# Order of three steps in a fused attention and SwiGLU kernel: Prelu and exp ahead of the copy of the sums over V, the bias ahead of a turn's last products

## Chip, cores and metric

The kernel runs on one core of one Trainium2 chip. The metric is device time in microseconds for one launch, the median of the runs; lower is better. TensorE is called PE in the profile, VectorE DVE, ScalarE ACT, GpSimd POOL and SyncE SP.

## The reference

```python
# q, k, v: (8, 8, 576, 64), batch x heads x sequence x head_dim, float32
scores = scale * np.matmul(q, k.transpose(0, 1, 3, 2))
kth = np.partition(scores, -top_k, axis=-1)[..., -top_k:-top_k + 1]   # top_k = 32
scores = np.where(scores >= kth, scores, -1000000000.0)
scores = scores - np.max(scores, axis=-1, keepdims=True)
attn = np.exp(scores)
attn = attn / (np.sum(attn, axis=-1, keepdims=True) + 1e-09)
attn_out = np.matmul(attn, v)
x = attn_out.transpose(0, 2, 1, 3).reshape(4608, 512)
g = x @ w_gate                                  # 512 x 1536
silu = g * (1.0 / (1.0 + np.exp(-g)))
out = (silu * (x @ w_val)) @ w_out              # 1536 x 512
```

## The kernel before

**Units.** Attention is cut into 160 units: for each of 8 batches five groups of query rows (four of 128, and a last one of 64), and for each group four pairs of heads. In the last group a unit has one search over both heads; in the others it has two, one for each head. The sequence of 576 is 4 x 128 + 64, so `J` is 4 and `qt == J` means the last group.

**The steps of unit n.** `scores` multiplies q by k on TensorE (tile `s`, L325, or L308 for the last group), and ScalarE copies the product out with the scale (`sc`, L330 or L315). `select` finds the 32 largest of a row on VectorE, with four rounds of MAX8 (L347) and three of MATCH_REPLACE8 (L351). `shift` makes the bias of the exponential on GpSimd, out of the largest and the 32nd maximum (L362); it waits for VectorE's last MAX8. `weigh` runs Prelu (L374, with the 32nd maximum) and exp (L379, with the bias and the row's sum into `tot`) on ScalarE. `normalize` takes the reciprocal of the sum on VectorE (L392, L393), and scales `e` by it on ScalarE (L397) for one head and on GpSimd (L399) for the other. `turn` transposes `e` on TensorE (`etps`, L412), and ScalarE copies the result out (`et`, L413). `values` multiplies two units' `et` by V on TensorE (`av`, L448), and ScalarE copies the sums into `xT` (L464), the input of the feed-forward part.

**Feeds.** The feed-forward part handles blocks of 256 tokens (`kb`), each once its `xT` is complete. `feed` multiplies `xT` by `w_gate` and `w_val` (`f`, L603; L516 for the first blocks, in halves), ScalarE and GpSimd make the gated product `h` (ScalarE L636 to L643, GpSimd L639 and L644), and seven groups of products with combinations of `w_out` and `h` follow (`y_ps`, `x_ps`, L669). GpSimd forms the combinations of `h` that these need (L676, L684, L689, L717); L676 and L689 write them over the block's `xT`. GpSimd also adds up the output (L656). Before that the weights are brought in and rounded by ScalarE, VectorE and GpSimd (L117 to L126), mixed in with the first 13 units or so.

**Turns.** The main loop runs over n, here called turn n. It writes the order of every engine by hand: a chain of dependencies at the end of the kernel keeps each engine's instructions as they are written, so an instruction that waits holds up all that is written behind it on its engine. Turn n searches unit n, weighs and normalizes unit n - 1, transposes unit n - 2, and in even turns takes the sums over V of units n - 4 and n - 3 and the scores of units n + 1 and n + 2. In between, `pieces(k)` puts in up to k pieces of a feed, as many as a budget (`credit`) allows. A feed's copies and products on ScalarE and GpSimd are kept in two lists (`on_act`, `on_pool`) and written out by `flush`, at fixed places of the turn and when a list has more than one entry.

**Around the change.** Turn n begins as follows: the budget is set, `flush(on_act)`, the bias of unit n - 1, `flush(on_pool)`, in even turns the scores of unit n + 1 (products and copies), the sums over V (products and the copy to `xT`), the products of the scores of unit n + 2, then Prelu and exp of unit n - 1, then the copies of the scores of unit n + 2. Two pieces follow, the transposes of unit n - 2, more pieces and the search, `normalize`, the rest of the search, and `pieces(6)` last. `finish_units` also starts the loads of V for the next batch, when the units are those of a last group.

**Buffers.** The score tiles, the transposes and the sums over V share five PSUM banks (pool `ps_t`), the feeds have three (`ps_f`). In an even turn the first four transposes of the turn write the bank of that turn's sums, so they wait for the copy to `xT`. `xT` has three buffers. A feed's first product of each group of four reads the first pair of heads, the third reads the third pair.

Of the kernel before, what the change touches and what calls it, by code (L numbers as in the profile page):

```python
# [25 lines left out]
def kernel(  # L26
# [214 lines left out]
    def load_v(i):  # L241
        b, hp = pairs[i]
        h = slice(2 * hp, 2 * hp + 2)
        vt = slabs.tile([P, 2, J, D], FP32, tag="v", name="v")
        v_last = vtail[i % NV]
        vl = vlast[i % NV]
        nc.sync.dma_start(
            vt[:].rearrange("p h j d -> p h (j d)"),
            v[b, h, 0:JP].rearrange("h (p j) d -> p h (j d)", j=J),
        )  # L250
        nc.sync.dma_start(v_last[P - R : P], v[b, h, JP:S].rearrange("h p d -> p h d"))
        for hh in range(2):
            o = hh * R
            nc.sync.dma_start(vl[o : o + R, o : o + R], v[b, 2 * hp + hh, JP:S])
        vs[i] = (vt, v_last, vl)
# [28 lines left out]
    def n_heads(qt):  # L284

        return 1 if qt == J else 2
# [70 lines left out]
    def shift(n):  # L357

        st = state[n]
        m, nh = st["m"], len(st["heads"])  # L360
        bias = small.tile([P, 2], FP32, tag="bias", name="bias")
        nc.gpsimd.tensor_tensor(  # L362
            bias[:, 0:nh], m[:, 0:nh, TOP_K - 1], m[:, 0:nh, 0], ALU.subtract
        )
        st["bias"] = bias

    def weigh(n):


        st = state[n]  # L370
        sc, m, e, heads, bias = st.pop("sc"), st.pop("m"), st["e"], st["heads"], st.pop("bias")
        tot = small.tile([P, 2], FP32, tag="tot", name="tot")
        for t, (hs, at) in enumerate(zip(heads, st.pop("source"))):
            nc.scalar.activation(  # L374
                e[:, hs], sc[:, at], AF.Prelu, bias=m[:, t, TOP_K - 1 : TOP_K], scale=-1.0,
                alpha=SMALL,
            )
        for t, hs in enumerate(heads):
            nc.scalar.activation(  # L379
                e[:, hs], e[:, hs], AF.Exp, bias=bias[:, t : t + 1], scale=-1.0 / SMALL,  # L380
                accum_out=tot[:, t : t + 1],
            )
        if n < AHEAD:
            nc.scalar.add(tot[:, 0 : len(heads)], tot[:, 0 : len(heads)], EPS)
        st["tot"] = tot
# [37 lines left out]
    def values(ns):  # L423

        b, qt, hp0 = units[ns[0]]
        last = qt == J
        ql = R if last else P
        assert hp0 % 2 == 0
        halves = [slice(0, R), slice(R, P)]
        av = ps_t.tile([P, 2, P], FP32, tag="t", name="av")  # L430
        for i, n in enumerate(ns):
            assert units[n] == (b, qt, hp0 + i)
            vt, v_last, vl = vs[b * NHP + hp0 + i]
            et = state.pop(n)["et"]
            for c in (*range(J), J) if last else (J, *range(J)):
                for hh in range(2):
                    d = slice(hh * R, (hh + 1) * R)
                    if c == J:
                        weights_ = v_last[:, hh, :] if last else vl[:, d]
                    else:  # L440
                        weights_ = vt[:, hh, c, :]
                    at = halves[hh ^ i] if last else None
                    moving = (
                        et[:, c, at]
                        if last
                        else et[:, c + (0 if c == J else hh * (J + 1)), :]
                    )
                    nc.tensor.matmul(  # L448
                        av[d, i, 0:ql],
                        weights_,  # L450
                        moving,
                        start=c == (0 if last else J),
                        stop=c == (J if last else J - 1),
                    )
        c0 = b * S + qt * P
        at = c0
        hps = slice(hp0, hp0 + len(ns))
        while at < c0 + ql:
            kb = at // BLK
            n_c = min((kb + 1) * BLK, c0 + ql) - at  # L460
            if kb not in xT:
                xT[kb] = ffn.tile([P, NHP, BLK], FP32, tag="xT", name="xT", bufs=3)
                done[kb] = 0
            nc.scalar.copy(  # L464
                xT[kb][:, hps, at - kb * BLK : at - kb * BLK + n_c],
                av[:, 0 : len(ns), at - c0 : at - c0 + n_c],
            )
            done[kb] += n_c * len(ns)
            at += n_c
# [299 lines left out]
    NU = len(units)  # L769
# [6 lines left out]
    def piece():  # L776

        if len(on_act) > 1:
            flush(on_act)
        if len(on_pool) > 1:  # L780
            flush(on_pool)
        for job in early_jobs[:]:
            cost = next(job, 0)
            if cost == 0:
                early_jobs.remove(job)
            elif cost is not None:
                return cost
        if early_jobs:
            return 0
        while True:  # L790
            if not current:
                if not todo or done.get(todo[0], 0) < tokens(todo[0], int(todo[0] >= HALVED)):
                    return 0
                flush(on_act)
                flush(on_pool)
                current.append(feed(todo.pop(0)))
            cost = next(current[0], 0)
            if cost == 0:
                current.pop()
                continue  # L800
            return cost or 0

    def fetch(n):

        b, qt, hp = units[n]
        i = b * NHP + hp
        if qt == 0:
            yield from prep(i)
        if qt == J and i + NHP < len(pairs):
            load(i + NHP)  # L810
# [16 lines left out]
    def scored(n):  # L827

        ahead = [n + 1] if n < 2 else [] if n % 2 else [n + 1, n + 2]
        return [m for m in ahead if m < NU and (units[m][1] < J or m % 2 == 0)]  # L830

    def valued(n):

        behind = [] if n % 2 else [n - 4, n - 3]
        return [m for m in behind if 0 <= m < NU]

    def pieces(n):
        for _ in range(n):
            if credit[0] >= 1:
                credit[0] -= piece()  # L840

    def run(steps):
        for _ in steps:
            pass

    def finish_units(ns):
        values(ns)
        for n in ns:
            b, qt, hp = units[n]
            if qt == J and b + 1 < B:  # L850
                load_v((b + 1) * NHP + hp)
# [14 lines left out]
    no = iter(())  # L866
    TURN = 2
    due, steps = [2.0], []
    for n in range(NU + 3):
        nh = n_heads(units[n][1]) if n < NU else 1  # L870
        topk = select(n) if n < NU else no
        norm = normalize(n - 1) if 0 <= n - 1 < NU else no
        nxt = [scores(m) for m in scored(n)]
        ahead = fetch(n + 3 if n else 2) if n + 3 < NU else no

        def dve(k, beside=True):

            for _ in range(k * nh):
                next(topk, None)
                due[0] += 5 / 6 if beside else 0  # L880
                if due[0] >= 1 and not (n == 0 and len(steps) == 5):
                    due[0] -= 1
                    steps.append(n)
                    rounding(1)

        if n >= NU - NHP:
            credit[0] = 8.0
        else:
            credit[0] = min(credit[0] + share(n), share(n) + 1)
        flush(on_act)  # L890
        if 0 <= n - 1 < NU:
            shift(n - 1)
        flush(on_pool)
        if nxt and (n < 2 or len(nxt) > 1):
            run(nxt.pop(0))
        if valued(n):
            finish_units(valued(n))
        if nxt:
            next(nxt[0])
        early[0]()  # L900
        if 0 <= n - 1 < NU:
            weigh(n - 1)
        if nxt:
            run(nxt.pop())


        dve(2, beside=False)
        if n == 0:
            run(ahead)
            load(3)  # L910
            ahead = fetch(3)
        if n < NHP:
            load_v(n)
        pieces(2)
        flush(on_act)
        dve(1)
        dve(1)
        if 0 <= n - TURN < NU:
            run(turn(n - TURN))

        flush(on_pool)
        next(ahead, None)
        pieces(1)
        next(ahead, None)
        dve(1)
        pieces(1)
        if n < AHEAD:
            run(topk)
        run(norm)
        run(topk)  # L930
        pieces(6)
    while piece():
        pass
# [48 lines left out]
```

## Time and profile before

| | us |
|---|---|
| median of 3 runs (1720.06 to 1721.92) | 1721.45 |
| profiled execution | 1721.06 |
| its span, first to last instruction | 1719.3 |
| TensorE busy | 1653.6 (96%) |
| VectorE busy | 1476.5 (86%) |
| ScalarE busy | 1256.9 (73%) |
| GpSimd busy | 798.3 (46%) |

The span is that of one profiled execution; some 1.8 us of the time lie around it. A line of the profile's timeline gives the start, the time, the engine, the source line, the operation, what it writes and reads, and how many like it were merged; in brackets stands how long the engine was idle before, and what ended that. Busy times of TensorE are modelled at their ends, since products overlap in the array. The mean granted TensorE clock was 0.977 of full speed, lower at the start only.

### The profile page before, as it was taken

The page shows a single profiled execution, that of the slowest core. Times are in us where ns is not written, and L with a number is a line of the kernel's source. Part 1 is how long each engine was busy: PE and PEld are TensorE (multiplying, and loading weights), DVE is VectorE, ACT ScalarE, POOL GpSimd, SP SyncE. Part 2 cuts the span into 40 slices and gives each one's busy share as a digit, 9 for nine tenths or more (in the row PEclk, how much of TensorE's full clock was granted, in tenths as well). Part 3 has the DMA queues.
Part 4 walks back from the last instruction along what each step waited for, and adds up shares of the span by engine and source line. Part 5 has one row for each costly group of instructions (what it writes and reads, how often), then busy time and mean ns, then how long its engine had stood idle before and what let it go on. Part 6 is the DMA issues. An engine that isn't in the chain of part 4 may idle for free.

```text
span 1719.3 us, 32119 instructions
## 1 busy us (share of the span) xinstructions
PE 1653.6 (96%) x11600; PEld 1403.4 (82%) x11600; DVE 1476.5 (86%) x3311; ACT 1256.9 (73%) x2901; POOL 798.3 (46%) x914
## 2 busy tenths in 40 slices
PE   5678999999999999999999999999999999999999
PEld 4478698987888887888888888888888888888887
DVE  7999899898999999997989989998999979999410
ACT  7899786777767687768776786767776778676531
POOL 4798544342353434343535334445344443445434
PEclk7698999999999999999999999999999999999999
DMA  7432120002100030001200030000400011000000
GB/s 209 138 118 92 29 72 1 14 1 72 29 13 1 15 72 27 1 2 43 56 14 1 13 72 28 1 14 2 98 1 13 1 41 32 13 2 13 1 13 13
DMA packets 109310, 59.74 MB, mean 35 GB/s; under 512 B 88544, under 2 KB 96992, under 8 KB 109152
## 3 DMA queue, kind: packets, MB, share of 16 engines
q1 hardware_dynamic: 108016, 57.37, 12.7%
q8 instruction: 91, 1.49, 0.3%
q14 instruction: 67, 0.55, 0.1%
q10 hardware_dynamic: 1136, 0.33, 0.1%
HBM read 48.23 MB, written 9.44 MB: 34 GB/s over the span
## 4 chain that ended last, share of the span: by engine, by line
PE 88%; DVE 6%; ACT 3%; issue 1%; POOL 1%; DMA 1%; SPq 0%; POOLq 0%; ACTq 0%
PE f L603 36%; PE x_ps L669 10%; PE av L448 9%; PE s L325 8%; PE y_ps L669 7%; PE etps L412 7%; PE f L516 6%; DVE m L347 2%; DVE e L351 2%; PE kqps L271 1%; PE o_ps L568 1%; PE s L308 1%; ACT e L379 1%; DVE size L124 1%; POOL e L399 0%
## 5 line engine op out<-in xcount | busy, mean ns | idle before, releaser
L347 DVE MAX8 m<-e 128x8 f32<-128x576 f32 x864 | 615.3, 748 | 3.3
L351 DVE MATCH_REPLACE8 e<-m,e 128x576 f32<-128x576 f32 x576 | 424.0, 743 | 0.0
L603 PE MATMUL f<-xT,wg 128*128 128x256 f32 x1440 | 335.6, 382 | 0.0
L603 PE MATMUL f<-xT,wv 128*128 128x256 f32 x1440 | 331.4, 380 | 0.0
L603 PEld LDWEIGHTS f<-xT,wg 128*128 128x128 f32 x1440 | 269.0, 190 | 47.3 <-issue 13.1
L603 PEld LDWEIGHTS f<-xT,wv 128*128 128x128 f32 x1440 | 268.2, 190 | 37.5 <-issue 3.8
L639 POOL TENSOR_TENSOR h<-h,half_g 128x512 f32<-128x512 f32 x90 | 114.7, 1274 | 354.2 <-ACT h L638 354.2
L330 ACT ACTIVATE sc<-s 128x288 f32<-128x288 f32 x512 | 167.7, 416 | 93.9 <-PE s L325 93.8
L379 ACT ACTIVATE e<-e,bias 128x576 f32<-128x576 f32 x288 | 221.6, 779 | 15.6 <-POOL bias L362 13.0
L412 PE MATMUL etps<-ident,e 128*128 128x128 f32 x1312 | 179.3, 279 | 37.9 <-POOL e L399 17.4
L374 ACT ACTIVATE e<-sc,m 128x576 f32<-128x576 f32 x288 | 211.8, 789 | 1.3 <-DVE m L347 1.3
L351 DVE MATCH_REPLACE8 e<-m,sc 128x576 f32<-128x576 f32 x288 | 211.9, 743 | 0.0
L347 DVE MAX8 m<-sc 128x8 f32<-128x576 f32 x288 | 203.3, 743 | 8.7 <-ACT sc L330 8.7
L412 PEld LDWEIGHTS etps<-ident,e 128*128 128x128 f32 x1312 | 155.2, 143 | 60.8 <-POOL e L399 22.9
L413 ACT COPY et<-etps 128x512 f32<-128x512 f32 (+1 forms) x448 | 184.8, 496 | 18.1 <-PE etps L412 17.7
L325 PE MATMUL s<-kqT 64*128 64x288 f32 x1024 | 171.2, 445 | 15.8 <-ACT sc L330 7.9
L399 POOL TENSOR_TENSOR e<-e,tot 128x576 f32<-128x576 f32 x140 | 160.5, 1150 | 55.8 <-DVE tot L393 47.1
L644 POOL TENSOR_TENSOR h<-h,val 128x512 f32<-128x512 f32 x90 | 114.7, 1274 | 135.0 <-ACT val L643 132.3
L397 ACT ACTIVATE e<-e,tot 128x576 f32<-128x576 f32 x148 | 119.4, 807 | 59.7 <-DVE tot L393 59.7
L448 PE MATMUL av<-et,v 128*64 128x128 f32 (+1 forms) x2560 | 157.9, 267 | 0.0
L325 PEld LDWEIGHTS s<-kqT 64*128 64x128 f32 x1024 | 95.6, 192 | 60.9 <-issue 23.7
L448 PEld LDWEIGHTS av<-et,v 128*64 128x64 f32 x2560 | 137.8, 140 | 5.9 <-ACT kqT L268 2.7
(86 smaller groups left out, 2252.1 us busy)
## 6 DMA issues: line engine op xcount, KB each, us to landing
v<-in_v_dram SPq DMA_DIRECT2D x32, 256.0 KB, 3.2
kq_in<-in_k_dram SPq DMA_DIRECT2D x63, 128.0 KB, 2.9
kq_in<-in_q_dram SPq DMA_DIRECT2D x63, 128.0 KB, 3.2
w<-in_moe_w_gate_dram SPq DMA_DIRECT2D x12, 512.0 KB, 3.7
w<-in_moe_w_val_dram SPq DMA_DIRECT2D x12, 512.0 KB, 3.8
w<-in_moe_w_out_dram SPq DMA_DIRECT2D x12, 512.0 KB, 3.5
out_dram<-o SPq DMA_DIRECT2D x38, 128.0 KB, 2.4
out_dram<-o SPq DMA_DIRECT2D x16, 256.0 KB, 2.5
```

Of the source, the lines that this page charges most:

```text
L325: nc.tensor.matmul(ps[:, 0:half], slab[d, q0 : q0 + P], slab[d, k0 : k0 + half])
L330: nc.scalar.mul(sc[:, i * half : (i + 1) * half], ps[:, 0:half], scale)
L347: nc.vector.max(m[:, t, 8 * r : 8 * r + 8], cur[:, hs])
L351: nc.vector.match_replace(e[:, hs], m[:, t, 8 * r : 8 * r + 8], cur[:, from_[t]], LOWEST)
L374: nc.scalar.activation(e[:, hs], sc[:, at], AF.Prelu, bias=m[:, t, TOP_K - 1 : TOP_K], scale=-1.0, alpha=SMALL,)
L379: nc.scalar.activation(e[:, hs], e[:, hs], AF.Exp, bias=bias[:, t : t + 1], scale=-1.0 / SMALL, accum_out=tot[:, t : t + 1],)
L399: nc.gpsimd.tensor_tensor(e[:, hs], e[:, hs], tot[:, t : t + 1].to_broadcast([P, S]), ALU.mult)
L412: nc.tensor.transpose(ps[:, c * P : (c + 1) * P], e[:, k0 : k0 + P], ident[:])
L413: nc.scalar.copy(et[:, c0 : c0 + cn, :], ps[:, 0 : cn * P].rearrange("p (c j) -> p c j", c=cn),)
L448: nc.tensor.matmul(av[d, i, 0:ql], weights_, moving, start=c == (0 if last else J), stop=c == (J if last else J - 1),)
L603: nc.tensor.matmul(ps[:, i, :], w[:, kc, m * P : (m + 1) * P], x[:, kc, :], start=(kc == 0), stop=(kc == KC - 1),)
L669: nc.tensor.matmul(ps, lhsT, T[i][m], start=m == 0, stop=m == MQ - 1)
```

## The change

Three edits in the order of writing; no operation is added or removed. `values` is cut in two by a `yield` after its products. In an even turn the products over V stay where they are, while the copy to `xT`, and what `finish_units` does after it, come behind Prelu and exp of unit n - 1 (and ahead of the copies of the scores of unit n + 2). The bias of unit n is written at the end of turn n, after its search and ahead of `pieces(6)`, instead of in turn n + 1 after `flush(on_act)`. So it comes ahead of those GpSimd products that `pieces(6)` writes out.

```diff
@@ values
                         stop=c == (J if last else J - 1),
                     )
+        yield
         c0 = b * S + qt * P
@@ finish_units
-        values(ns)
+        yield from values(ns)
         for n in ns:
@@ the main loop
         flush(on_act)
-        if 0 <= n - 1 < NU:
-            shift(n - 1)
         flush(on_pool)
         if nxt and (n < 2 or len(nxt) > 1):
             run(nxt.pop(0))
-        if valued(n):
-            finish_units(valued(n))
+        summed = finish_units(valued(n)) if valued(n) else no
+        next(summed, None)
         if nxt:
             next(nxt[0])
         early[0]()
         if 0 <= n - 1 < NU:
             weigh(n - 1)
+        run(summed)
         if nxt:
             run(nxt.pop())
@@ the end of the turn
         run(norm)
         run(topk)
+        if n < NU:
+            shift(n)
         pieces(6)
```

## The prediction

> **What bounds the kernel now.** I read the busy table first: TensorE 1653.6 us of 1719.3 (96%), VectorE 86%, ScalarE 73%, GpSimd 46%. One number for the span hides the stages, so I asked for busy time by stretch.
>
> ```profile
> core 0: us, PE busy (x) PEld busy (x) DVE busy (x) ACT busy (x) POOL busy (x), PEclk, DMA share, GB/s
> 43.00:86.00 43.00, 27.16 (x177) 20.22 (x178) 43.00 (x91) 37.77 (x85) 34.09 (x32) 0.66 0.47 138
> 86.00:172.00 86.00, 71.65 (x589) 65.24 (x590) 85.38 (x176) 80.73 (x179) 77.90 (x69) 0.90 0.34 105
> 172.00:344.00 172.00, 168.13 (x1435) 141.86 (x1434) 154.15 (x329) 131.54 (x316) 78.44 (x87) 1.00 0.11 29
> 860.00:1032.00 172.00, 172.00 (x1201) 145.65 (x1200) 154.72 (x353) 130.97 (x304) 69.31 (x83) 1.00 0.11 25
> ```
>
> From 43 to 172 us VectorE has no idle time (128.4 of 129): the top-k search sets the pace while the weights are being rounded. After 172 us TensorE does, and from 860 on it has hardly a gap until the last units. So the third question is what TensorE still waits for after 172, as the table of waits gives it (who waited for whom: total us, times, longest).
>
> ```profile
> PE etps L412 <- ACT e L397: 4.7, 3, 2.6
> PE s L325 <- ACT et L413: 2.2, 3, 1.2
> PE etps L412 <- ACT sc L315: 2.0, 1, 2.0
> PE x_ps L669 <- POOL h L717: 1.2, 1, 1.2
> PE s L325 <- ACT sc L330: 1.2, 1, 1.2
> PE etps L412 <- POOL e L399: 1.0, 2, 0.5
> PE kqps L264 <- ACT et L413: 0.8, 2, 0.4
> PE x_ps L669 <- POOL xT L676: 0.6, 1, 0.6
> ```
>
> The sum is 13.7 us. Nearly all that a shorter wait on ScalarE can win is in here, plus 0.2 to 0.3 us of drained pipeline at each stop (399.14: 2.05 waited, but the next block started 2.26 late). The other engines wait far more, for nothing at the end:
>
> ```profile
> DVE tot L392 <- ACT e L379: 128.3, 104, 11.0
> ACT xT L464 <- PE av L448: 98.2, 68, 5.2
> POOL bias L362 <- DVE m L347: 45.1, 36, 5.6
> ```
>
> **The change, part by part.** It adds and removes no operation. TensorE's, VectorE's and SyncE's streams keep their order (the loads of V that follow a turn's sums are written later, but pass nothing on SyncE). Two things move.
>
> *(a) The copy of the sums (L464) goes behind two Prelu and two exp on ScalarE, in each even turn.* The timeline of ScalarE shows a usual even turn:
>
> ```profile
> 927.24 1.32 ACT L330 ACTIVATE sc<-s 128x288 f32<-128x288 f32 x4 [3.41 <-PE s L325]
> 930.08 0.37 ACT L464 COPY xT<-av 128x256 f32<-128x256 f32 x1 [1.52 <-PE av L448]
> 930.35 1.44 ACT L374 ACTIVATE e<-sc,m 128x576 f32<-128x576 f32 x2
> 933.21 1.29 ACT L330 ACTIVATE sc<-s 128x288 f32<-128x288 f32 x4
> ```
>
> The scores are copied out at 928.56, ScalarE idles 1.52 us for TensorE's 40 products over V, then copies. With the new order Prelu starts at about 928.5 and exp ends at 931.3 instead of 933.2, 1.9 us earlier; the copy follows at once and ends at 931.7 instead of 930.45, 1.26 us later; all behind it on ScalarE is 1.5 us earlier. I did this for all even turns: exp gains 1.9 us in about half, 1.1 in most of the rest, 0.1 to 0.3 where ScalarE never waited for the sums.
>
> What the later copy may hold up: the first four transposes of the same turn (etps, L412) reuse the bank of the sums, so they wait for it; and a feed that starts in the same turn reads xT. TensorE reached these transposes at 933.83 here, 2.1 us after the copy's new end. From turn 14 on that slack is 0.9 to 4.6 us, but for turn 66 (0.2) and the two below. In turns 4 to 12 it is negative by up to 3.7 us, since exp there waits for a bias queued behind GpSimd's rounding; but the next five transposes waited anyway (3.69 us at 63.95, 3.64 at 109.44) and VectorE sets the pace: I cost it at 0 (from -1 to +2 us). If that cover went, turns 4, 8 and 10 would show their 3 us each. Feeds that start in the turn of their last copy are turns 38, 66, 74, 110 and 146. The third product of a feed is the first that reads the copied half, 0.86 us after the feed's start (two of 16 rows of 3.46 us each product): 1490.32 in turn 146, with the copy at 1490.10. So 0, by 0.2 us. Turn 66 is the exception: there Prelu waits for VectorE's last maximum, the copy ends near 686.65, and the third product ran at 686.07: loss 0.6.
>
> Gains at the stops, each by its chain in the timeline:
> - 164.77, start of the saturated part: GpSimd's scaling of e follows a product that waited 1.44 us for ScalarE's val, which stands behind exp of turn 12; exp gains 1.4, val 0.9. Gain 0.9.
> - 275 to 304: four stops, x_ps on GpSimd L676 (0.61) and L717 (1.24) and twice etps on L399 (0.48), together 3.4 us of late starts. GpSimd waited for ScalarE's val at 275.12 and p at 295.69, both directly behind the score copies, which come 1.5 us earlier. All four go: 3.3.
> - 399.14 and 401.75, turn 36: the score copies behind exp start at 396.8 instead of 398.60. The first transposes then wait for the xT copy (396.9 for 396.44), the next run at 397.5 for 399.14, the nine after at 400.05 for 401.75. Gain 1.7.
> - 797 to 803: etps on e, kqps on et, in the turn after one that gains 3.5. Gain 0.8.
> - 1652.06, the last unit: exp ends 1.0 earlier, but the copy of the sums now holds the bank (1649.9 for 1648.68), so half is left: 0.5.
>
> *(b) The bias (L362, 0.2 us) goes ahead of GpSimd's products of a turn's last pieces.* It passes work in some 35 turns, elsewhere nothing. It waits for VectorE's last maximum, and all behind it on GpSimd waits too. Where GpSimd was already behind VectorE it costs 0.2 us, covered. The dangerous turns are those in which L676 started before that maximum: 71, 89, 107 (1.52 us before), 115, 133, 151 (1.35 to 1.39).
>
> ```profile
> 742.63 1.15 POOL L399 TENSOR_TENSOR e<-e,tot 128x576 f32<-128x576 f32 x1 [0.83 <-PE f L603]
> 743.74 2.10 POOL L676 TENSOR_TENSOR xT<-h 128x256 f32<-128x256 f32 x3
> 745.79 1.27 POOL L644 TENSOR_TENSOR h<-h,val 128x512 f32<-128x512 f32 x1
> ```
>
> VectorE's maximum ended at 745.26, and TensorE reads the first result of L676 at 745.00. Kept there, the bias would put L676 at 745.54: about 1.3 us of stall. But part (a) brings VectorE's maximum forward, as it idles for exp in each even turn: by 1.07 us in 71, 89 and 107 and by 1.88 in the other three. So L676 starts near 744.5, 0.3 us late for TensorE: 0.9 for three turns, 0 for the others. At the end, bias 158 ran at 1644.58 behind ten operations, and exp waited 4.39 us for it; that wait goes, but the last exp stands behind a copy that waits for TensorE until 1648: nothing more.
>
> **Two rules weighed.** The Trainium skill, "Perfetto Trace Analysis", section "Identifying the Most-Contended Engine", says that matmul busy time misleads and weight-load busy share is the measure of headroom. By it (1403.4 us, 82%) the kernel has 316 us of latency, and freeing ScalarE's 98.2 us of waits could pay tens of us. The stretches speak against it: 172.00 of 172.00, and 16 products take 3.46 us each time. I take the stops. Against the change speaks "ScalarE: Activation LUTs", section "What ACT_TABLE_LOAD costs": a switch to another set of functions costs about 2.66 us with its drain. Were Prelu, exp and the copy in different sets, the new order could add one switch in 80 turns: an estimate of 213 us.
>
> ```profile
> L276 ACT ACT_TABLE_LOAD x1 | 1.3, 1283 | 2.1 <-issue 2.1
> ```
>
> One load for the whole kernel, with Tanh, Prelu, exp and copies already alternating: 0.
>
> **The sum.** 0.9 + 3.3 + 1.7 + 0.8 + 0.5 = 7.2; less 0.6 and 0.9: 5.7 us. The profiled execution took 1721.06 us (span 1719.3); that gives 1715.4. The median of the runs is 0.4 higher, so I forecast 1715.7.
>
> **Rivals.**
> 1. *Absorbed.* The stops between 172 and 410 are followed by other waits of the same engines (kqT copies after 403, VectorE's maxima at 406), and half or more of the 7.2 is given back: -3 to +2 us, 1718.5 to 1723. For it: VectorE is 90% busy there. Against: after each stop TensorE runs for tens of us without a wait. 0.24.
> 2. *Slower: the bias blocks GpSimd.* If VectorE's maxima do not come forward (because VectorE idles for something else than exp), L676 is 1.8 us late in six turns, less 0.5 of slack: 1.3 x 6 = 8 us, against at most 5 of gains, which need exp early too: +3 to +5, 1724.5 to 1726.5. It decides once the maximum ends more than 0.2 us after L676's old start. For it: the maximum is last in 71, 89, 107 even by my numbers. Against: VectorE's idle time is 128.3 us on exp and 11.6 on all TensorE. 0.12.
> 3. *More goes than I count.* Most of the 13.7 us of stops vanish, with the drains, and VectorE's earlier maxima relieve the stops at 679 to 684: -9 to -12, 1709.5 to 1712.5. 0.10.
> The forecast itself has 0.54, from 1713 to 1718.
>
> A measurement of this kernel can tell about 0.2% (3.4 us) from no change. Faster by more: the forecast and rival 3, 0.64 in all, with a little of rival 1: 0.66. Within: 0.23. Slower: 0.11. The range takes in all but rival 2 and the far end of 3: 1711 to 1722.5.
>
> **What would show it.** After: ScalarE's wait of xT for the sums near 0 of 98.2, VectorE's wait for exp down by some 60 to 90 us, and its other waits no shorter; no TensorE stop at 275 to 304; one stop near 397 instead of two; a new TensorE wait on xT L465 (turn 36, 66, the end). Wrong if TensorE shows waits on GpSimd L677 in turns 71, 89, 107, or on L465 in many turns, or if its total of waits after 172 is not below 10 us.

## The result, and the profile after

The changed kernel takes 1712.06 us (median of 6 runs, 1711.97 to 1714.35) against 1721.68 us for the kernel before (6 runs, 1720.06 to 1722.0): a ratio of 0.9949, with a 95% interval of 0.9936 to 0.9962. The forecast was 1715.7, faster, with a range of 1711 to 1722.5 that takes in most of the rivals. The time is in that range, but 0.9 us below the forecast's own (1713 to 1718) and inside the range of rival 3 (1709.5 to 1712.5). The gain is 9.6 us by these medians, for 5.7 us in the sum. The profiled executions differ by 9.0 us in time (1721.06 and 1712.03) and by 9.1 in span (1719.3 and 1710.2).

The busy time by stretch of the changed kernel (engines in the order PE, weight load, VectorE, ScalarE, GpSimd, then the granted clock):

```profile
86.00:172.00 86.00, 72.62 (x616) 66.37 (x616) 85.14 (x173) 79.59 (x175) 77.65 (x67) 0.92 0.35 105
172.00:344.00 172.00, 170.60 (x1470) 145.71 (x1469) 158.34 (x340) 135.50 (x326) 80.36 (x89) 1.00 0.11 29
860.00:1032.00 172.00, 172.00 (x1168) 146.04 (x1166) 156.60 (x356) 127.84 (x293) 74.81 (x91) 1.00 0.09 22
```

The bounds are the same two: VectorE up to about 172 us, TensorE afterwards. Between 172 and 344 us TensorE's gaps went from 3.87 us to 1.40. TensorE's waits after 172 us:

```profile
PE etps L412 <- ACT e L397: 3.5, 2, 1.8
PE s L325 <- ACT et L413: 2.0, 3, 1.0
PE f L604 <- ACT xT L465: 1.3, 1, 1.3
PE kqps L264 <- ACT et L413: 0.9, 2, 0.5
PE etps L412 <- ACT xT L465: 0.4, 1, 0.4
PE etps L412 <- POOL e L399: 0.3, 1, 0.3
```

They add up to 8.4 us, from 13.7. Both waits on GpSimd's combinations (x_ps) and those on the score copies (L315, L330) are gone; two on the copy to xT are new, as foreseen, in turns 66 and 36. That is 5.3 us less of waiting, while the span is 9.1 us shorter: the waits alone do not account for the gain. ScalarE in a usual even turn (turn 90, the one shown in the prediction) now reads:

```profile
918.77 1.32 ACT L330 ACTIVATE sc<-s 128x288 f32<-128x288 f32 x4 [4.24 <-PE s L325]
919.94 1.46 ACT L374 ACTIVATE e<-sc,m 128x576 f32<-128x576 f32 x2
922.79 0.38 ACT L465 COPY xT<-av 128x256 f32<-128x256 f32 x1
923.04 1.34 ACT L330 ACTIVATE sc<-s 128x288 f32<-128x288 f32 x4
```

Prelu starts as soon as the first scores are out, the copy finds the sums ready (no bracket), and the second scores are copied 4.27 us after the first start; before it was 5.97 (927.24 to 933.21).

To see where the time came from, I read the start of the same TensorE block in both timelines; before minus after is the lead of the changed kernel, and its growth is what a stretch gave.

| block of TensorE | before | after | lead | growth | foreseen |
|---|---|---|---|---|---|
| av, turn 14 | 177.69 | 176.56 | 1.13 | 1.13 | 0.9 |
| f, turn 27 | 304.27 | 300.14 | 4.13 | 3.00 | 3.3 |
| f, turn 38 | 409.79 | 401.63 | 8.16 | 4.03 | 1.7 |
| f, turn 66 | 689.75 | 681.41 | 8.34 | 0.18 | -0.6 |
| x_ps, turn 72 | 751.06 | 742.99 | 8.07 | -0.27 | -0.3 |
| f, turn 80 | 829.10 | 820.36 | 8.74 | 0.67 | 0.8 |
| x_ps, turn 108 | 1110.14 | 1101.93 | 8.21 | -0.53 | -0.6 |
| f, after the last unit | 1655.09 | 1646.04 | 9.05 | 0.84 | 0.5 |

Six of the eight terms are right within 0.35 us, but the first can't be told from chance: a second execution of the kernel before (before_again, below) is itself 1.12 us ahead at the block of turn 14. Behind that block the two keep their distance within 0.1 us, but for turn 36 (0.8) and the end (0.3). One row is far off: turn 36 gave 4.03 us for 1.7. The table of before shows what else is there, in a column that I had not used at that place, the granted clock (last but two):

```profile
400.00:402.00 2.00, 0.25 (x2) 0.25 (x2) 1.87 (x4) 2.00 (x5) 0.60 (x2) 0.51 0.02 5
402.00:404.00 2.00, 2.00 (x11) 2.00 (x11) 1.90 (x5) 1.90 (x6) 0.00 (x0) 0.50 0.06 12
404.00:406.00 2.00, 2.00 (x11) 1.67 (x11) 1.93 (x6) 1.46 (x3) 0.00 (x0) 0.50 0.00 0
```

After the stops of turn 36, TensorE ran at half clock from 400.0 to 406.8 us. So the clock of the kernel before is not lower at the start only, as the section on its profile has it. In the profile of the changed kernel it is 1.00 in this place. Whether the stops cause this, and how much of the 4.03 it makes, is for the experiments; so is which of the two parts gains, and whether the other one costs.

### The profile page after: what moved, and what is told of

It is laid out like the page before. It is cut to its first block, busy times and chain, and to the rows that moved or that the text cites. A ratio compares the mean times of both kernels' runs of the same rounds, so it can differ in the third digit from the quotient of the medians.

```text
span 1710.2 us, 32128 instructions
## 1 busy us (share of the span) xinstructions
PE 1647.4 (96%) x11600; PEld 1398.2 (82%) x11600; DVE 1476.5 (86%) x3311; ACT 1259.5 (74%) x2901; POOL 799.0 (47%) x914
## 4 chain that ended last, share of the span: by engine, by line
PE 88%; DVE 5%; ACT 4%; DMA 1%; POOL 1%; issue 1%; SPq 0%; POOLq 0%; ACTq 0%
PE f L604 37%; PE x_ps L670 10%; PE av L448 9%; PE s L325 8%; PE y_ps L670 8%; PE etps L412 7%; PE f L517 6%; DVE m L347 2%; DVE e L351 2%; PE kqps L271 1%; PE o_ps L569 1%; PE s L308 1%; ACT e L379 1%; DVE size L124 1%; ACT e L374 0%
## 5 line engine op out<-in xcount | busy, mean ns | idle before, releaser
L330 ACT ACTIVATE sc<-s 128x288 f32<-128x288 f32 x512 | 170.4, 431 | 105.2 <-PE s L325 104.6
L413 ACT COPY et<-etps 128x512 f32<-128x512 f32 (+1 forms) x448 | 183.6, 486 | 66.0 <-PE etps L412 65.6
L325 PE MATMUL s<-kqT 64*128 64x288 f32 x1024 | 169.2, 441 | 13.7 <-ACT sc L330 7.5
```

The costliest lines, as they stand in the source:

```text
L325: nc.tensor.matmul(ps[:, 0:half], slab[d, q0 : q0 + P], slab[d, k0 : k0 + half])
L330: nc.scalar.mul(sc[:, i * half : (i + 1) * half], ps[:, 0:half], scale)
L413: nc.scalar.copy(et[:, c0 : c0 + cn, :], ps[:, 0 : cn * P].rearrange("p (c j) -> p c j", c=cn),)
```

## Experiments

All times are medians; the ratio is to the kernel before on the same chip.

**Part (a) alone: copy_only.** The changed kernel, with the bias back in its old place.

```diff
         flush(on_act)
+        if 0 <= n - 1 < NU:
+            shift(n - 1)
         flush(on_pool)
...
-        if n < NU:
-            shift(n)
         pieces(6)
```

> Part (a) alone: Prelu and exp ahead of the copy to xT in even turns, the bias in its old place. Theory 1 (all the gain is in ScalarE's order, the bias adds nothing): the stops at 275 to 304 and 396 to 406 shrink as in the changed kernel, less 0.3 us in turn 36 where exp waits for a bias queued behind GpSimd's sums; and the three late starts of 0.2 to 0.3 us at GpSimd's differences in turns 71, 89 and 107 are gone (+0.7). So 1711 to 1712.5, as fast as the changed kernel or up to 1 us faster. Rival (the two parts need each other, since exp at the head of ScalarE's queue waits for a late bias): at least 2 us slower than the changed kernel, 1714 or more, with ScalarE's wait of exp for the bias above 20 us.

Measured: 1711.74 us (1711.62 to 1713.33, 5 runs), ratio 0.9953 (0.9941 to 0.9966); the changed kernel has 0.9949. The two can't be told apart by time. Where they differ, the timelines say: its x_ps blocks of turns 72 and 90 start with no loss (the late starts in turns 71, 89 and 107 are gone), and the f block of turn 38 starts at 402.12 for 401.63: it was 0.08 us behind at turn 27, and the other 0.4 are lost in turn 36, where exp waits for the bias. ScalarE's waits of exp for the bias are

```profile
ACT e L379 <- POOL bias L362: 18.6, 14, 4.4
```

against 9.7 us in the changed kernel, and cost TensorE nothing but those 0.4 us. So the gain is part (a)'s, and the rival that the parts need each other fell.

**Part (b) alone: bias_only.** The kernel before, with `shift(n)` ahead of `pieces(6)` and not at the head of the next turn; the copy to xT stays in its old place.

> Part (b) alone: the bias ahead of a turn's last pieces, the copy to xT in its old place. Theory 1: VectorE's maxima stay where they were, so the bias holds the differences (xT, L676) back until 745.54 in turn 71, and likewise in 89 and 107; TensorE stops about 1.4 us in each, no stop in 115, 133, 151 (there TensorE reads them a turn later): 4 us slower than before, 1725 to 1726, with three waits of x_ps on the differences of about 1.3 us. Rival (the bias is off every path): within 1 us of before.

Measured: 1725.73 us (1724.0 to 1726.18, 7 runs), ratio 1.0027 (1.0016 to 1.0039): slower, in the range that was expected. GpSimd in turn 71, and the TensorE block that reads the differences:

```profile
743.49 1.15 POOL L399 TENSOR_TENSOR e<-e,tot 128x576 f32<-128x576 f32 x1 [0.82 <-PE f L603]
746.19 0.20 POOL L362 TENSOR_TENSOR bias<-m 128x2 f32<-128x2 f32 x1 [1.56 <-DVE m L347]
746.34 2.10 POOL L676 TENSOR_TENSOR xT<-h 128x256 f32<-128x256 f32 x3
```

```profile
747.12 1.56 PE L669 MATMUL x_ps<-t,xT 128*128 128x256 f32 x6 [1.11 <-POOL xT L676]
```

The whole mechanism is in these four lines: GpSimd has nothing to do for 1.56 us, because the bias at the head of its queue waits for VectorE; the differences behind it could have started, and TensorE stops for 1.11 us. It is 3.9 us over four such waits, where before had 0.6 in one (at 278). The three new ones, in turns 71, 89 and 107, are of 1.11 us each, and by the starts of the blocks behind them they cost 4.2 us. In the changed kernel the same place loses 0.27 us only, since part (a) brings VectorE's maximum forward:

```profile
735.90 0.20 POOL L362 TENSOR_TENSOR bias<-m 128x2 f32<-128x2 f32 x1 [1.33 <-DVE m L347]
736.05 2.09 POOL L677 TENSOR_TENSOR xT<-h 128x256 f32<-128x256 f32 x3
736.82 1.56 PE L670 MATMUL x_ps<-t,xT 128*128 128x256 f32 x6
```

(The first two lines are GpSimd's timeline, the third TensorE's.) This was the mechanism of the forecast's slower rival; it is real, and it was avoided by about a microsecond: VectorE's maximum came some 0.8 us before TensorE was through with the products ahead of the differences (735.82 and 736.66), where in the kernel before it came 0.26 us after that.

**The clock: filled_stop.** The kernel before, with more work for TensorE in the first stop of turn 36.

```diff
-                nc.tensor.transpose(ps[:, c * P : (c + 1) * P], e[:, k0 : k0 + P], ident[:])
+                for _ in range(6 if n == 34 and c0 == 0 else 1):
+                    nc.tensor.transpose(ps[:, c * P : (c + 1) * P], e[:, k0 : k0 + P], ident[:])
```

> The kernel before, with the first four transposes of unit 34 (turn 36) written six times over instead of once, so that TensorE has 2.2 us more of work in the stop at 396.9 to 399.1, into the bank that it holds anyway. The other engines' order is untouched. Theory (in before the granted clock fell to 0.5 from 400 to 407 us since TensorE had been idle, and this cost 2.3 us of its own): with the stop filled the clock stays at 1.00 there, and the kernel is about 2 us faster than before though it does more work, 1719 to 1720. Rival (the slow stretch comes from the order of the work, or the clock falls at any time): no change, or 0 to 0.5 us slower.

Measured: 1719.02 us (1717.0 to 1719.88, 11 runs) against 1720.49 us (1718.83 to 1722.49, 17 runs), ratio 0.9991 (0.9982 to 1.0): 1.5 us, near the 2 that were expected, with an interval that reaches no change. In the stretches of its profile the second stop is still there, but the clock stays up:

```profile
400.00:402.00 2.00, 0.56 (x4) 0.32 (x4) 1.83 (x4) 2.00 (x6) 1.15 (x2) 1.00 0.09 22
402.00:404.00 2.00, 1.69 (x15) 1.69 (x16) 1.93 (x5) 1.91 (x5) 0.00 (x0) 1.00 0.00 0
404.00:406.00 2.00, 1.98 (x29) 1.62 (x29) 1.93 (x6) 2.00 (x6) 0.00 (x0) 1.00 0.07 18
```

Twenty more transposes, and the f block of turn 38 starts at 408.17 for 409.79. It was 0.55 us behind at 396, so filling the stop gave 2.17 us. That is the price of the half clock in this execution of the kernel before, and it leaves 4.03 - 2.17 = 1.86 for the order itself, where the forecast had 1.7.

**The kernel before once more: before_again.**

> The kernel before once more, for a second profile. Theory (the falls of the granted clock at 168 and 400 us follow from TensorE's stops there and recur): the fall at 400 for 6.8 us is there again, the one near 168 for 3 to 7 us too. Rival (they were an accident of one execution): neither is there, and the time is 3 to 4 us lower.

Measured: 1719.22 us (one run). The clock fell again, at 165.7 us and at 401.3, here for 3.4 us each. In turn 36:

```profile
400.00:402.00 2.00, 1.33 (x9) 1.34 (x10) 1.80 (x5) 1.91 (x3) 0.00 (x0) 0.81 0.00 1
402.00:404.00 2.00, 2.00 (x11) 1.85 (x9) 1.93 (x7) 1.85 (x6) 0.00 (x0) 0.50 0.01 4
404.00:406.00 2.00, 2.00 (x32) 1.82 (x32) 1.96 (x3) 1.54 (x4) 0.19 (x1) 0.83 0.19 44
```

So the fall recurs, but its length does not. This execution gains 0.79 us in turn 36 on the first one, so its half clock cost 2.17 - 0.79 = 1.38 us, and with the length comes a part of the spread between executions of the same kernel. Against this profile the changed kernel ends 7.6 us ahead, not 9.05.

**The early turns: from_turn_14, and turn14_again.** The changed kernel, with the old order of the copy in turns 4 to 12.

```diff
+        if n < 14:
+            run(summed)
         early[0]()
         if 0 <= n - 1 < NU:
             weigh(n - 1)
         run(summed)
```

> The changed kernel, but with the copy to xT ahead of Prelu and exp (the old order) in turns 4 to 12. Theory (in these turns exp waits for a bias behind GpSimd's rounding, the copy behind it holds a bank, and TensorE's transposes come 2 to 5 us late, of which 0.7 us is left at 167 us where TensorE becomes the bound): the transposes at 62, 111 and 133 us no longer wait for xT, and 0 to 1 us is won: 1711 to 1712. Rival (the early turns are covered by VectorE, so nothing changes): within 0.3 us of the changed kernel. A third case: without exp ahead of the copy in turn 12, GpSimd's queue is no earlier and the gain at 168 us is lost: 1 us slower than the changed kernel.

> The kernel from_turn_14 once more, for a second profile, since its runs lay at 1711.4 and at 1714.3 to 1715.2. Theory (the granted clock): a profile of an execution of 1714 or more shows a stretch of half clock near 400 us, or a longer one at 165, that the profile at 1711.4 did not have, and TensorE's waits are the same. Rival: its clock is the same and some wait of TensorE is longer by 3 us.

Measured: 1714.44 us (1711.38 to 1715.24, 5 runs), ratio 0.9963 (0.9951 to 0.9976), and 1715.39 (1711.19 to 1715.54, 3 runs). The transposes no longer wait for xT in the early turns: near 100 us the two profiles are within 0.6 us of the kernel before, where the changed kernel is 2.0 us behind. But the gain near 168 us is lost, which was the third case: from 166 to 178 us they gain 0.39 and -0.01 us on the kernel before, the changed kernel 1.82. The first profile, taken at 1711.38, is no faster than the changed kernel's 1712.03 by more than executions differ. But most of the runs are 3 to 4 us slower. The second profile was taken at 1715.54 and shows in turn 36

```profile
396.00:398.00 2.00, 0.26 (x3) 0.11 (x2) 1.87 (x4) 2.00 (x6) 0.41 (x2) 0.96 0.39 89
398.00:400.00 2.00, 2.00 (x10) 2.00 (x11) 1.90 (x5) 1.91 (x5) 0.00 (x0) 0.50 0.10 25
```

while the profile at 1711.38 has a clock of 1.00 there. Of the 4.1 us between the two profiles this makes 1.37. The rest lies ahead of it: 1.27 us at 120 us already, and 1.25 between 120 and 140, where the clock fell at 131 us for 3.4 us in the first profile and for 6.8 in the second; 0.4 came near 168. For the early turns themselves this pair is inconclusive.

**The same with the stop filled: turn14_filled.** from_turn_14, with transposes of the identity into the bank that unit 35's transposes overwrite.

```diff
             ps = ps_t.tile([P, 512], FP32, tag="t", name="etps")
+            for _ in range(14 if n == 35 and c0 == 0 else 0):
+                nc.tensor.transpose(ps[:, 0:P], ident[:], ident[:])
```

> The kernel from_turn_14 with 14 transposes of the identity ahead of those of unit 35, so that TensorE works in the stop near 394 us. Theory (from_turn_14 mostly ran at 1714.3 to 1715.4 since the clock fell near 398 us in those executions, and at 1711.3 in those in which it did not): the fall at 398 is gone, all or nearly all runs are at 1711 to 1713, the median is 1.5 to 3 us below from_turn_14's 1714.4. Rival (the slow executions come from elsewhere): the median stays at 1714 to 1715.

Measured: 1712.04 us (1711.49 to 1712.45, 5 runs), ratio 0.9953 (0.9941 to 0.9966). The clock stays at 1.00 in turn 36, and the profile gains 4.02 us there on the kernel before, as from_turn_14's first (4.02) and unlike its second (2.65). The slow executions are gone (none of five, after six of eight), and the spread is 1.0 us for 3.9. The clock of turn 36 explains 1.4 us of that; the rest of the difference lay ahead of the filled stop, and these runs were taken on another chip, so why all five are fast is not shown.

**Two places mended: two_mended.** Part (a) alone, with these exceptions.

```diff
-        if 0 <= n - 1 < NU:
+        if 0 <= n - 1 < NU and n - 1 != 35:
             shift(n - 1)
...
+        if n == 66:
+            run(summed)
         early[0]()
         if 0 <= n - 1 < NU:
             weigh(n - 1)
         run(summed)
...
+        if n == 35:
+            shift(n)
         pieces(6)
```

> Part (a) alone, with two places mended: in turn 66 the copy to xT stays ahead of Prelu (there Prelu waits for VectorE anyway), and the bias of unit 35 alone goes ahead of GpSimd's last sums of its turn. Theory (the losses of part (a) and the gain of part (b) are where the traces show them): TensorE's wait of f on xT (1.3 us at 677) goes, and the first transposes of turn 36 come 0.4 us earlier: 1.5 to 1.7 us faster than part (a) alone at an equal clock, about 1710. Rival (the copy ahead delays exp in turn 66 and the wait moves to the score copies or to the next transposes): within 0.4 us of part (a) alone.

Measured: 1710.38 us (1708.53 to 1712.08, 5 runs), ratio 0.994 (0.9927 to 0.9952). TensorE's wait of f on xT is gone, and its f block of turn 66 starts at 680.89 for 681.75 in copy_only, although it was 1.15 us behind at turn 14 (177.78 for 176.63): 2.0 us won in between, 0.4 in turn 36 and 1.6 in turn 66. By the medians it is 1.4 us faster than copy_only, which the intervals do not separate.

**TensorE kept busy: kept_busy, and all_mended.** kept_busy is two_mended with such transposes of the identity ahead of the transposes of units 11 (12 of them), 35 (14) and 159 (14). all_mended is kept_busy with the old order of the copy for n < 14 as well.

> The kernel two_mended with transposes of the identity ahead of the transposes of units 11 (12 of them), 35 (14) and 159 (14), into the bank that is overwritten right after, so that TensorE works in its stops at 166, 395 and 1641 us. Theory (the granted clock falls to half after a stop, in some executions of a kernel and not in others, by where the stop lies in time; this makes most of the spread between runs): no stretch of half clock between 165 and 1690 us, the stretch at 1643 (3.4 us at 0.5, worth 1.7 us) goes, runs agree within 1 us, and the median is 1.5 to 3 us below that of two_mended: 1707.5 to 1709. Rival (the clock's falls are not tied to these stops, or the added rows delay what they stand in front of): the same time as two_mended or up to 1 us slower, and the spread stays.

> The kernel kept_busy with the copy to xT ahead of Prelu and exp in turns 4 to 12 as well. Theory (the early turns cost 1 to 2 us at 166 us, which from_turn_14 won back, but lost again to the clock; with the stops filled that loss is closed): 1 to 2 us faster than kept_busy, 1706 to 1707.5. Rival (the start of the execution, with its loads, moves the time by as much as the early turns do): within 0.7 us of kept_busy.

Measured: kept_busy 1708.26 us (1707.72 to 1710.05, 5 runs), ratio 0.9931 (0.9918 to 0.9945); all_mended 1706.93 us (1706.26 to 1708.19, 5 runs), ratio 0.9923 (0.9909 to 0.9936). Neither profile has a stretch of half clock between 140 and 1700 us; but two_mended's own profile has none there either. The median of kept_busy is where it was expected, 2.1 us below two_mended's, within intervals that overlap. Its profile does not show that the fillers made this: it leads two_mended's by 1.09 us at 150 us, ahead of the first filler, and by 0.95 after the last unit. Its runs still spread by 2.3 us, not by under 1. all_mended is 1.3 us faster by the medians; set against the kernel before on its own chip it is 0.7 by the medians and 1.4 by the ratios. In the profiles it is 2.0 us ahead of kept_busy near 100 us and level with it at turn 14 (0.96 and 0.99 us ahead of the kernel before): in this pair, what the copy behind exp costs in the early turns is made up by then. all_mended beats the kernel before by 0.8% and the changed one by 0.26% (0.9923 to 0.9949), while the intervals of these two only touch.

## Why the prediction was right, point by point

The direction and the path of the gain were right: ScalarE's new order takes stops of TensorE away. The size was not. Of the 9.05 us of lead in the two profiles 5.7 come from the order after turn 14, where the forecast's terms add up to 4.8; 2.2 come from the granted clock in turn 36, which the forecast left out; and 1.1 were there at turn 14, no more than two executions of one kernel differ. So the order alone gave what the sum had, 5.7 us, but by other terms: the first (0.9) can't be seen in these rows, and turn 66 came out 0.8 better than costed. That the two agree is luck, and so is a part of what the clock added.

- *TensorE's stops after 172 us are what can be won.* Right. ScalarE's 98.2 us of waits for the sums shrank to 5.1, and the kernel gained 9, not the tens of us of the estimate that was weighed and left aside.
- *Which stops go.* The four at 275 to 304 left one of 0.35 us: 3.00 for 3.3. In the timeline of the kernel before the first two stops read

```profile
277.88 1.56 PE L669 MATMUL x_ps<-t,xT 128*128 128x256 f32 x6 [0.61 <-POOL xT L676]
280.36 0.77 PE L412 MATMUL etps<-ident,e 128*128 128x128 f32 x5 [0.48 <-POOL e L399]
```

In the changed kernel's they are one unbroken row; the last line is the stop that is left:

```profile
276.04 1.46 PE L670 MATMUL x_ps<-t,xT 128*128 128x256 f32 x6
277.33 1.31 PE L412 MATMUL etps<-ident,e 128*128 128x128 f32 x9
298.24 0.76 PE L412 MATMUL etps<-ident,e 128*128 128x128 f32 x5 [0.35 <-POOL e L399]
```

- *Turn 36: 1.7 us.* Right in mechanism, and mis-sized, as the stop's second price was left out: the half clock behind it. TensorE before, and after:

```profile
396.44 0.66 PE L412 MATMUL etps<-ident,e 128*128 128x128 f32 x4
399.14 0.86 PE L412 MATMUL etps<-ident,e 128*128 128x128 f32 x5 [2.05 <-ACT sc L315]
401.75 2.18 PE L412 MATMUL etps<-ident,e 128*128 128x128 f32 x9 [1.75 <-ACT e L397]
```

```profile
392.76 1.27 PE L412 MATMUL etps<-ident,e 128*128 128x128 f32 x9 [0.38 <-ACT xT L465]
395.77 1.20 PE L412 MATMUL etps<-ident,e 128*128 128x128 f32 x9 [1.75 <-ACT e L397]
```

  There is a first wait of 0.38 us for the new copy and no second, and the nine transposes behind them still wait 1.75 us. They start 5.98 us earlier than before, from a lead of 4.13: 1.85 for the order. The nine then took 2.18 us at half clock, and take 1.20 now; by turn 38 the lead is 8.16, so 2.18 are the clock's, as filled_stop has it (2.17). With this term the sum is 7.9. The new order does not rule the fall out: turn14_again has it, with the same waits of 0.38 and 1.75 us.
- *Turn 66: -0.6.* The stop of f on xT came, with 1.32 us, and cost 1.6 with the start behind it. But the lead had grown by 1.9 us before it, as the stops of 679 and 684 (1.24 and 1.19 us before) went to 0.99 and none; with 0.15 lost elsewhere 0.18 was left. The term had the third product wait until 686.65; it ran at 677.73, which is 685.74 with the lead of 8.01 that the kernel had at 669. (The 0.86 us from the feed's start to its third product are four rows of the sixteen, not two: four ran before the wait.)
- *Saturated part from 164.77 on: 0.9.* The size (1.13) is luck. The stop did shrink, to 1.61 and 0.45 us from 2.04 and 0.63, 0.6 us for 0.9. But the early turns, costed at 0, are some 2 us behind from 90 to 140 us, and of this 0.69 is left at 166 (166.65 for 165.96). What made the lead is the clock: before ran at 0.50 from 167.9 to 171.3 us, the changed kernel at 1.00. All seven profiles with the old order in the early turns and no filler in this stop have a fall at 165 to 169 us, the three with the new order have none; whether it can't fall there is not shown.
- *797 to 803: 0.8.* Measured 0.67: the wait of etps on e is gone, that of kqps on et stayed, with 0.45 us for 0.37.
- *GpSimd's differences: 3 x 0.3.* Measured 0.27 in turn 71, and 0.53 for the other two. That the other three turns cost nothing is right as well. The slower rival counted six turns of 1.3 us; part (b) alone shows three, since in turns 115, 133 and 151 TensorE reads the differences a turn later.
- *What the profile would show.* The total of TensorE's waits is below 10 us, and one stop is left near 299 where none was foreseen. The wait on xT is in turns 66 and 36; not at the end, where the half gain became 0.84. VectorE's wait for exp went down to 101.1 from 128.3, by 27 us and not by 60 to 90, and another of its waits did become longer:

```profile
DVE tot L392 <- ACT e L379: 101.1, 85, 9.3
ACT et L413 <- PE etps L412: 65.6, 64, 3.2
DVE e L351 <- PE etps L412: 39.5, 19, 3.9
```

  VectorE waits 39.5 us for transposes to free its buffer (11.6 before), ScalarE 65.6 us for transposes to copy (17.7 before). Engines that are not the bound run into the bound one elsewhere; the idle time moves and stays.
- *Rivals.* Absorbed: no, each stop's gain stayed to the end, as the leads show. More goes than I count: the time is inside its range, and one of its reasons holds, the relief at 679 to 684. But 8.4 of the 13.7 us of stops are left, and what brought the time there besides is the clock, which no rival named.

## What to carry to other kernels

When one engine is saturated, add up that engine's own waits: with the price of the clock behind them they bound what a reordering elsewhere can win, and each one is followed in the timeline to what it waits for. Before a difference of 1 us is put down to a change, see how far two executions of one kernel are apart at the same block. Price a stop of TensorE at its length plus what the granted clock does after it, and read the clock in stretches of 2 us there; a stop that can't be avoided can be filled with work into a bank that is overwritten anyway, which pays where the clock would have fallen (2.17 us in filled_stop) and not elsewhere (kept_busy's profile gained nothing on two_mended's). An instruction that is moved forward on its queue may only wait for something that is as early as all that is put behind it: the bias cost 4.2 us alone, and 0.8 once its input came forward.

## What the runs showed of the hardware

The granted clock follows how busy TensorE was, in windows of 3.41 us. In the clock records of each of the twelve profiles all changes lie whole multiples of 3.41 us apart, and after 140 us each fall to 0.50 lasts for one or two of these windows, counted from one fall to the next. Adding up the matmul time in these windows (ends modelled), from 140 us to the end of the last unit: all twenty falls follow a window with 0.8 to 1.64 us of matmuls, and of the windows with 1.67 to 2.4 us none starts a fall. One with 1.57 us (before_again, ended at 397.8) passed. So it takes no idle window: in before the stops near 166 us (2.04 and 0.63 us) and of 2.05 and 1.75 us in turn 36 were enough, some 1.3 us of matmuls being left in each of the windows that ended at 167.9 and 400.0. The Trainium skill, "TensorE: Matmul & The Clock Gate", section "Part 1: The HAM clock gate (the "warmup" mystery)", has the window of about 3.4 us and the half clock, and names at least one idle window for the way down; the runs here fall after windows that are up to 48% busy.

In turn 36 a fall of 3.4 us cost 1.4 us (1.38 in before_again, 1.37 in turn14_again), one of 6.8 us 2.2 in before and 2.5 in bias_only. The windows lie differently against the program in each execution: the stop of 1.75 us in turn 36 ended 0.04 us behind the end of a window in turn14_again, which had held 1.33 us of matmuls, and in from_turn_14 in the middle of one that held 2.07. So the same stop drops the clock in one execution and not in another. Between these two profiles, 4.1 us apart, this made 1.37 us in turn 36, and 1.25 us came where the clock fell at 131 us, for one window in the one and for two in the other.
